# Storing the query projections of later batches ahead of their batches, one of them through the keys' buffer

## The chip, the cores and the metric

The kernel runs on one core of a Trainium2 chip. The metric is the device time of one execution in microseconds (us), the median of several runs. A core has five engines with an instruction queue each, in order: TensorE (PE, matmuls), VectorE (DVE), ScalarE (ACT), GpSimd (POOL) and SyncE (SP), which here issues nearly all DMA transfers. An engine whose next instruction waits holds up everything queued behind it on that engine, and on SyncE that means transfers that could have gone.

## The reference

Two blocks follow each other. The first is a linear attention with sketched features for 4 batches of 4 heads, 1088 positions and 32 dimensions; the second is a mixture of 8 experts over the 4352 rows (4 x 1088) that come out of it, weighted by 8 rounds of a row and column normalisation.

```python
def phi(x):                                   # S1, S2: 8 x 32
    a = einsum('rd,bhsd->bhsr', S1, x)
    b = einsum('rd,bhsd->bhsr', S2, x)
    return einsum('bhsi,bhsj->bhsij', a, b).reshape(..., 64)
q_p, k_p = phi(q), phi(k)
kv = einsum('bhsf,bhsd->bhfd', k_p, v);  z = sum(k_p, axis=2)
x = einsum('bhsf,bhfd->bhsd', q_p, kv) / (einsum('bhsf,bhf->bhs', q_p, z) + 1e-6)
# x as (4352, 128): batch and position x head and dimension
P = exp(x @ w_gate - max)
for _ in range(8):
    P /= P.sum(1) + 1e-9;  P /= P.sum(0) + 1e-9;  P *= N / E
out = sum over e of P[:, e] * (maximum(x @ w1[e], 0) @ w2[e])
```

## The kernel before

**Attention.** Batch 0 takes a short way of its own: its query features are made by two matmuls that repeat both factors in PSUM (`query_products`, `multiply`), and sums and quotients follow in three chunks of positions (`fractions`, `divide`). Batches 1 to 3 go through DRAM. `transpose_q(b)` turns the loaded queries in 32x32 blocks on VectorE into the single buffer `qT`. `queries_ab(b)` multiplies `qT` with both sketches (L418, 12 records on TensorE, into two PSUM banks), ScalarE copies the product to `qab` (one buffer, L421), and SyncE stores it to DRAM twice: as `qa` (L425) and as `qb` (L429). `repeat_a(b)` reads `qa` back, each row repeated, into `ph` (two buffers, batch b uses `phs[b % 2]`, L434), and `repeat_b(b)` reads `qb` back into `rb` (one buffer, L437). `times(b, c)` multiplies the two on VectorE, in thirds (L444), `tops(b, c)` contracts them with the sums of the keys on TensorE (L453, L457), and `over(b, c)` divides on VectorE. `take_over(b, ...)` then stores the result to DRAM (`xd<-xt`, L477) and reads it back in its other layout into `xT` (`xT<-xd`, L479), from where the experts take it.

The keys take a similar way without DRAM: `transpose_k(b)` into `kT` (L292, L294), `keys_ab(b)` (L303, L307, TensorE and a ScalarE copy), `keys_products(b, part)` on VectorE (L319), `keys_sums(b)` on TensorE (L335), `keys_kept(b)` into `kvs`.

**Experts.** The first layer is a step of two matmuls into one bank of PSUM (`first`, L889) and a ReLU on ScalarE (L893) into `hb`; a step's two halves run beside each other on TensorE. VectorE forms differences of hidden blocks (L906), and the second layer follows eight steps later (`into`, L1062); 7 products stand for 8 block products, or 20 for a larger form, in the way of fast matrix multiplication. The unweighted work of experts 0 and 1 runs first, group by group: 16 steps each on columns of batch 0 (256, 288 and 256 wide), then three groups of width 480 that start with the columns of batch 1, and so on; all others wait for the routing weights.

**What sets the order.** `fill(n)` lays down expert steps from a generator until n units are spent (a unit is a step of 480 columns; a step of 256 is 0.533). Attention and routing are written out by hand with `fill` between their parts, under a manual order for VectorE and TensorE, and at the very start for ScalarE too:

```python
def fill(n):
    owed[0] += n
    while owed[0] > 0.25:
        owed[0] -= next(work)
...
        for b in range(1, B):
            for n, _ in zip((1.4,) * (9 if b + 1 < B else 5), attention(b), strict=True):
                fill(n)
```

After the start, ScalarE and SyncE are ordered by a scheduler, so what stands ahead of what on these two follows from when it supposes things to be ready. Four PSUM banks (tag `a`) serve first-layer steps, `tops`, the keys and the query projections alike. A program-wide set of eight DMA semaphores is used in turn, and a transfer waits for the one that used its semaphore before.

Of the kernel before, what the change touches and what calls it, by code (L numbers as in the profile page):

```python
# [10 lines left out]
F32 = mybir.dt.float32  # L11
# [39 lines left out]
def kernel(  # L51
# [12 lines left out]
    nc = tc.nc  # L64
    P = nc.NUM_PARTITIONS
# [59 lines left out]
    xT = big.tile([P, N + 2 * 32], F32, name="xT")  # L125

    W9 = 9 * 32
    qT = wk.tile([P, 4 * W9], F32, name="qT", bufs=1)
    nc.gpsimd.memset(qT[:, S:], 0.0)
    kT = wk.tile([P, S], F32, name="kT", bufs=1)  # L130

    phs = [wk.tile([P, 2, 4 * W9], F32, name=f"ph{i}", bufs=1) for i in range(2)]
    rb = wk.tile([P, 2, 4 * W9], F32, name="rb", bufs=1)

    lgT = qT[:, 0:S].rearrange("p (a s) -> p a s", s=32)
    lgp = kT.rearrange("p (a e) -> p a e", e=32)
    pT = dram.tile([E, N], F32, name="pT")


# [24 lines left out]
    def load_q(b):  # L164
        qx = ld.tile([P, SA, D], F32, tag="q", name="qx")
        nc.sync.dma_start(out=qx, in_=q[b].rearrange("h (s a) d -> (h s) a d", a=SA))
        loaded["q", b] = qx

    def load_v(b):
        vx, o = v_slots[b % 2], v[b].offset  # L170
        for c in range(4):
            nc.sync.dma_start(
                out=vx[32 * c:32 * (c + 1), 0:H, 0:NT, :].rearrange("p h t d -> p h (t d)"),
                in_=AP(tensor=v.tensor, offset=o + NT * D * c, ap=[[SA * D, 32], [S * D, H], [1, NT * D]]))
        for c in range(2):
            nc.sync.dma_start(
                out=vx[32 * c:32 * (c + 1), 0:H, NT, :],
                in_=AP(tensor=v.tensor, offset=o + (4 * NT + c) * D, ap=[[SA * D, 32], [S * D, H], [1, D]]))

    load_k(0)  # L180
    load_q(0)
    load_v(0)

    def load_w(e, sums=True, again=False):
        w1 = wpool.tile([P, F], F32, tag="w1", name="w1")
# [92 lines left out]
    nc.gpsimd.memset(wg, 0.0)  # L278
    nc.sync.dma_start(out=wg[:, 0:E], in_=moe_w_gate)
    first_w = load_w(0)  # L280
    load_q(1)
    load_v(1)


    keys, queries = {}, {}

    def transpose_q(b, lo=0, hi=S):
        nc.vector.transpose(out=qT[:, lo:hi], in_=loaded["q", b].rearrange("p a d -> p (a d)")[:, lo:hi])

    def transpose_k(b):  # L290
        kx = loaded["k", b]
# [50 lines left out]
    def keys_kept(b):  # L342
        pv = sums_of.pop(b)
        for s in range(2):
            sl = slice(64 * s, 64 * (s + 1))
            if b:
                x, y = kvs[b % 2][sl, :, s, :], pv[sl].rearrange("p i c d -> p i (c d)")[:, :, 0:D + 1]
            else:
                x, y = kvz[sl, :, :, s, :], pv[sl].rearrange("p i c d -> p c i d")
            if s:  # L350
                nc.vector.tensor_copy(x, y)
            else:
                nc.scalar.copy(x, y)
# [55 lines left out]
    def queries_ab(b):  # L409
        qa = dram.tile([H * R, 2, 2, 2 * W9], F32, name=f"qa{b}")  # L410
        qb = dram.tile([2, R, 2 * R, 2, 2 * W9], F32, name=f"qb{b}")
        ab = wk.tile([P, 3, 192], F32, tag="qab", name="qab", bufs=1)
        x = qT.rearrange("p (h q c t s) -> p h c t q s", h=2, q=2, c=3, t=3)
        for cs in ((0, 1), (2,)):
            pq = bank()[:, 0:192 * len(cs)].rearrange("p (c n) -> p c n", n=192)
            for i, c in enumerate(cs):
                for s in range(2):
                    nc.tensor.matmul(pq[64 * s:64 * (s + 1), i].rearrange("p (t q s) -> p t q s", t=3, q=2),  # L418
                                     wdq.rearrange("p n f -> p (n f)"), x[:, s, c], start=True, stop=True,
                                     tile_position=(0, 64 * s))  # L420
            nc.scalar.copy(ab[:, cs[0]:cs[-1] + 1], pq)  # L421
        abf = ab.rearrange("p c n -> p (c n)")
        for s in range(2):
            x = abf[64 * s:64 * s + 32].unsqueeze(1).to_broadcast([32, 2, 2 * W9])
            nc.sync.dma_start(out=qa[:, :, s], in_=x)  # L425
        for s in range(2):
            for h in range(2):
                x = abf[64 * s + 32 + h:64 * (s + 1):2].unsqueeze(1).to_broadcast([2 * R, R, 2 * W9])
                nc.sync.dma_start(out=qb[h, :, :, s].rearrange("i f n -> f i n"), in_=x)  # L429
        queries[b] = qa, qb  # L430

    def repeat_a(b):
        for j in range(4):
            nc.sync.dma_start(out=phs[b % 2][j::4], in_=queries[b][0].rearrange("(x r) j s n -> (r j) x (s n)", x=2))  # L434
# [11 lines left out]
    def tops(b, c):  # L446

        pn = bank()[:, 0:3 * H * (D + 1)].rearrange("p (t h d) -> p t h d", t=3, h=H)
        ph = third(phs[b % 2], c)
        for t in range(3):  # L450
            for i in range(2):
                for s in range(2):
                    nc.tensor.matmul(pn[64 * s:64 * (s + 1), t, 2 * i:2 * i + 2].rearrange("p h d -> p (h d)"),  # L453
                                     ph[:, i, s, 64 * t:64 * (t + 1)], kvs[b % 2][:, i].rearrange("p h d -> p (h d)"),
                                     start=(t == 0 and i == 0), stop=False, tile_position=(0, 64 * s))
        for s in range(2):
            nc.tensor.matmul(pn[64 * s:64 * (s + 1), :, :, D], ones[:, 0:64], eps, start=False, stop=True,  # L457
                             tile_position=(0, 64 * s))
        queries[b, c] = pn
# [14 lines left out]
    def take_over(b, lo, hi):  # L474

        xd = dram.tile([P, H, hi - lo], F32, name=f"xd{b}{lo}")
        nc.sync.dma_start(out=xd, in_=turned[b][:, :, lo:hi])  # L477
        for h in range(H):
            nc.sync.dma_start(  # L479
                out=xT[32 * h:32 * (h + 1), b * S:b * S + 4 * W9].rearrange("d (f n) -> d f n", f=4)[:, :, lo:hi],  # L480
                in_=xd.rearrange("(f d) h n -> h d f n", f=4)[h])
# [16 lines left out]
    def attention(b):  # L498


        follows = b + 1 < B
        keys_sums(b)
        times(b, 0)
        if follows:
            transpose_q(b + 1)
        yield
        keys_kept(b)
        if follows:
            queries_ab(b + 1)
            repeat_a(b + 1)  # L510
        times(b, 1)
        tops(b, 0)
        yield
        times(b, 2)
        if follows:
            repeat_b(b + 1)
        over(b, 0)
        tops(b, 1)
        yield
        over(b, 1)  # L520
        if b + 1 == B:
            take_over(b, 0, 192)
        yield
        tops(b, 2)
        if follows:
            transpose_k(b + 1)
        if b + 2 < B:
            load_k(b + 2)
            load_q(b + 2)
            load_v(b + 2)  # L530
        yield
        over(b, 2)
        if b + 1 < B:
            take_over(b, 0, W9)
        else:
            take_over(b, 192, W9)
        if follows:
            keys_ab(b + 1)
            yield
            keys_products(b + 1, 0)  # L540
            yield
            keys_products(b + 1, 1)
            yield
            keys_products(b + 1, 2)
            yield
# [589 lines left out]
    with tc.manual_schedule(engines={engines.DVE, engines.PE, engines.Activation}):  # L1135
        st = projections()
        transpose_k(0)
        keys_ab(0)
        repeated(st)
        load_k(1)  # L1140
        transpose_q(0, 0, chunks[0][1])
        query_products(0)
        for part_ in range(3):
            keys_products(0, part_)
        keys_sums(0)
        multiply(0)
        transpose_q(0, chunks[0][1])
        keys_kept(0)
        query_products(1)
        fractions(0)  # L1150
        multiply(1)
        divide(0)
        fractions(1)
        query_products(2)
        divide(1)
    with tc.manual_schedule(engines={engines.DVE, engines.PE}):
        fill(1)
        multiply(2)
        fractions(2)
        fill(1)  # L1160
        transpose_q(1)
        queries_ab(1)
        repeat_a(1)
        repeat_b(1)
        fill(1)
        divide(2)
        fill(1)
        transpose_k(1)
        load_k(2)
        load_q(2)  # L1170
        load_v(2)
        fill(1)
        keys_ab(1)
        fill(1.5)
        keys_products(1, 0)
        fill(1.5)
        keys_products(1, 1)
        fill(1.5)
        keys_products(1, 2)
        fill(1.5)  # L1180
        for b in range(1, B):
            for n, _ in zip((1.4,) * (9 if b + 1 < B else 5), attention(b), strict=True):
                fill(n)
        for n in routing():
            fill(n)
        early.close()
        pools.append(ctx.enter_context(tc.tile_pool(name="late", bufs=2)))
        prepare_x(PLAIN)
        fill(8)
# [32 lines left out]
```

## Time and profile before

| | |
|---|---|
| time, median of 3 | 937.68 us (936.96 to 938.76) |
| span of the profiled execution | 935.3 us, TensorE clock 0.998 |
| TensorE (PE) busy | 914.8 us |
| VectorE (DVE) busy | 696.3 us |
| ScalarE (ACT) busy | 416.6 us |
| moved by DMA | 128.14 MB, mean 137 GB/s |
| `rb<-qb`, 1152 KB, issue to landing | 8.0 us (median of 3) |
| `qx<-in_q`, 544 KB | 5.3 us |
| `xT<-xd`, 144 KB | 3.3 us |

Busy times are sums over the span, and the ends of matmuls are modelled, so a busy TensorE need not be at its peak. A line of a timeline gives the start, the length, engine and line of the kernel, what is written from what, the count, and in brackets the idle time before it and what ended it. A wait for several things is put down to the one that came last by the profile, which can be the wrong one where a DMA was among them.

### The profile page before, as it was taken

To read this page: it belongs to the slowest core of one execution; us is meant where nothing else is said; L and a number is where in the kernel's file an instruction comes from. 1 tells how busy PE (TensorE), PEld (TensorE's weight loads), DVE (VectorE), ACT (ScalarE), POOL (GpSimd) and SP (SyncE) were. 2 spreads that over 40 slices of the span, in tenths; PEclk is the share of its full clock that TensorE was granted. 3 is DMA by queue.
4 is the path that set the end of the run, shared out by engine and by line. 5 is a ranking of instruction groups with operands and counts; after the bars stand their busy time and mean duration, and the time that the engine had idled before them with its cause. 6 is when DMAs were issued, how large, how long until landed. Compare 5 with 4: busy or idle time off the path is not lost.

```text
span 935.3 us, 18858 instructions
## 1 busy us (share of the span) xinstructions
PE 914.8 (98%) x7434; PEld 556.6 (60%) x7434; DVE 696.3 (74%) x1200; ACT 416.6 (45%) x901; POOL 195.9 (21%) x182
## 2 busy tenths in 40 slices
PE   8888999999999999999999999999999999999997
PEld 6676634666666666665555555555555555556864
DVE  7687769978788788586876656965757977768655
ACT  2544345564444454434544444544445444445443
POOL 2010000073665501130020101201110343321210
PEclk9999999999999999999999999999999999999999
DMA  7896300123335545354354534364434446442640
GB/s 216 226 290 166 113 21 1 26 105 108 107 109 170 172 148 151 121 174 142 117 154 121 179 107 148 111 182 131 140 115 152 151 150 204 160 167 92 183 140 12
DMA packets 93208, 128.14 MB, mean 137 GB/s; under 512 B 25376, under 2 KB 71456, under 8 KB 88384
## 3 DMA queue, kind: packets, MB, share of 16 engines
q1 hardware_dynamic: 91888, 126.78, 43.8%
q8 instruction: 58, 0.95, 0.4%
q10 hardware_dynamic: 1232, 0.16, 0.1%
q14 instruction: 30, 0.25, 0.1%
HBM read 107.88 MB, written 19.05 MB: 136 GB/s over the span
## 4 chain that ended last, share of the span: by engine, by line
PE 90%; DVE 8%; issue 1%; ACT 1%; POOL 0%; DVEq 0%; ACTq 0%; POOLq 0%
PE a L889 47%; PE s L1062 40%; DVE hb L906 2%; PE a L335 1%; PE a L114 1%; PE a L303 0%; PE a L453 0%; DVE rs L582 0%; DVE ph L444 0%; DVE p L585 0%; DVE cs L588 0%; DVE kp L319 0%; DVE kept L715 0%; DVE w L718 0%; DVE kT L292 0%
## 5 line engine op out<-in xcount | busy, mean ns | idle before, releaser
L889 PE MATMUL a<-xe,w 128*64 128x256 f32 (+1 forms) x2560 | 517.5, 470 | 0.0
L893 ACT ACTIVATE hb<-a 128x256 f32<-128x256 f32 (+5 forms) x408 | 194.9, 479 | 253.5 <-PE a L889 225.0
L893 ACT ACTIVATE hx<-a 128x256 f32<-128x256 f32 (+1 forms) x360 | 167.1, 464 | 213.9 <-PE a L889 194.1
L889 PEld LDWEIGHTS a<-xe,w 128*64 128x64 f32 x2560 | 206.8, 137 | 79.8
L1062 PE MATMUL s<-hb,ws 128*64 128x256 f32 (+4 forms) x1344 | 237.8, 395 | 2.4 <-DVE hb L906 1.6
L1062 PE MATMUL s<-hx,ws 128*64 128x256 f32 x1280 | 204.8, 379 | 0.6 <-DVE kept L718 0.6
L951 DVE TENSOR_TENSOR hb<-hb 128x512 f32<-128x512 f32 (+1 forms) x204 | 133.4, 665 | 93.9 <-ACT hb L893 89.8
L951 DVE TENSOR_TENSOR hx<-hx 128x512 f32<-128x512 f32 (+1 forms) x204 | 153.3, 761 | 66.3 <-ACT hx L893 61.1
L658 POOL TENSOR_TENSOR xe<-xT,xe 128x768 f32<-128x768 f32 (+2 forms) x41 | 85.1, 2076 | 554.5 <-DMA xe<-pT 401.6
L1062 PEld LDWEIGHTS s<-hb,ws 128*64 128x64 f32 x1344 | 113.8, 137 | 110.6 <-issue 80.0
L1062 PEld LDWEIGHTS s<-hx,ws 128*64 128x64 f32 x1280 | 105.9, 137 | 99.7 <-issue 74.4
L889 PE MATMUL a<-xT,w 128*64 128x480 f32 (+4 forms) x512 | 119.4, 463 | 3.7 <-DVE hb L906 2.5
L1062 PE MATMUL s<-hb,w 128*64 128x256 f32 (+4 forms) x496 | 101.9, 410 | 0.0
L906 DVE TENSOR_TENSOR hb<-hb 128x480 f32<-128x480 f32 (+8 forms) x96 | 64.2, 670 | 21.1 <-ACT hb L893 13.6
L1062 PE MATMUL s<-hx,w 128*64 128x256 f32 x384 | 68.3, 379 | 0.0
L889 PEld LDWEIGHTS a<-xT,w 128*64 128x64 f32 x512 | 50.5, 137 | 26.6 <-issue 14.2
L238 POOL TENSOR_TENSOR ws<-w 128x256 f32<-128x256 f32 (+1 forms) x70 | 60.1, 892 | 13.6 <-PE a L889 8.7
L1062 PEld LDWEIGHTS s<-hb,w 128*64 128x64 f32 x496 | 45.8, 137 | 22.8 <-issue 8.1
L906 DVE TENSOR_TENSOR hx<-hx 128x256 f32<-128x256 f32 (+1 forms) x65 | 39.1, 607 | 24.5 <-ACT hx L893 23.4
L951 DVE TENSOR_TENSOR pqg<-hb 128x512 f32<-128x512 f32 x68 | 48.8, 759 | 0.0
L1062 PEld LDWEIGHTS s<-hx,w 128*64 128x64 f32 x384 | 34.0, 137 | 10.9 <-DVE hx L906 0.3
L951 DVE TENSOR_TENSOR pqg<-hx 128x512 f32<-128x512 f32 x68 | 35.8, 566 | 0.0
(164 smaller groups left out, 468.8 us busy)
## 6 DMA issues: line engine op xcount, KB each, us to landing
w<-in_moe_w_dram SPq DMA_DIRECT2D x82, 512.0 KB, 5.0
ws<-ws SPq DMA_DIRECT2D x34, 1024.0 KB, 4.9
xe<-pT SPq DMA_DIRECT2D x34, 384.0 KB, 4.0
ws<-ws SPq DMA_DIRECT2D x12, 512.0 KB, 4.9
qb<-qab SPq DMA_DIRECT2D x12, 288.0 KB, 4.2
ph<-qa SPq DMA_DIRECT2D x12, 288.0 KB, 4.4
rb<-qb SPq DMA_DIRECT2D x3, 1152.0 KB, 8.0
pb<-pT SPq DMA_DIRECT2D x6, 384.0 KB, 6.7
```

The source lines that it names most:

```text
L114: nc.tensor.matmul(warm[:, 0:P], ones, ones, start=True, stop=True)
L238: tc.keep_in_program_order(nc.gpsimd.tensor_tensor(ws[:, c:c + len(ns)], blocks(x), blocks(y), op=Alu.subtract if off else Alu.add))
L335: nc.tensor.matmul(pv[64 * s:64 * (s + 1), i], kp[0:n, H * t + h].rearrange("p i j -> p (i j)"), vx[0:n, slots[h], t, :], start=(t == 0 an ...
L658: tc.keep_in_program_order(nc.gpsimd.tensor_tensor(out, x, pb, op=Alu.mult))
L889: nc.tensor.matmul(ph[sl], loaded_w[j][0][:, P * f + H2 * s:P * f + H2 * (s + 1)], sources[j][:, lo:hi], start=True, stop=True, tile_posit ...
L893: nc.scalar.activation(out=out, in_=ph, func=Act.Relu)
L906: nc.vector.tensor_tensor(out, a, b, op=Alu.subtract)
L951: nc.vector.tensor_tensor(out if not isinstance(out, tuple) else places(*out), places(*a), places(*b) if isinstance(b, tuple) else b, op=A ...
L1062: nc.tensor.matmul(sums[g][i][H2 * s:H2 * (s + 1), n * place:n * (place + 1)], w, x, start=c == 1, stop=c == per, tile_position=(0, H2 * s))
```

## The change

Before, the queries of batch b+1 were transposed, projected and stored during attention(b), and those of batch 1 after the last chunk of batch 0 had been multiplied. Now:

- q1 is loaded right after batch 0's data, ahead of the first expert's weights; q2 and q3 are loaded as soon as the two `qx` buffers come free.
- The queries of batch 1 are transposed into `kT`, which is idle between the keys of batch 0 and those of batch 1, and are projected, stored and read back during batch 0.
- The queries of batch 2 are transposed and projected between the key products of batch 1; those of batch 3 in the middle of attention(1), two yields apart.
- With that, the keys of batch 1 come earlier too, and the expert work laid before attention(1) shrinks from 11 units to 5.5.

It is meant to have the data of `ph` and `rb` in place before `times` asks for them.

```diff
-    qT = wk.tile([P, 4 * W9], F32, name="qT", bufs=1)
-    nc.gpsimd.memset(qT[:, S:], 0.0)
-    kT = wk.tile([P, S], F32, name="kT", bufs=1)
+    qT, kT = (wk.tile([P, 4 * W9], F32, name=n, bufs=1) for n in ("qT", "kT"))
+    for t in (qT, kT):
+        nc.gpsimd.memset(t[:, S:], 0.0)
...
     load_k(0)
     load_q(0)
     load_v(0)
+    load_q(1)
...
     first_w = load_w(0)
-    load_q(1)
     load_v(1)
...
     def transpose_q(b, lo=0, hi=S):
-        nc.vector.transpose(out=qT[:, lo:hi], in_=...)
+        to = kT if b == 1 else qT
+        nc.vector.transpose(out=to[:, lo:hi], in_=...)
...
-        x = qT.rearrange("p (h q c t s) -> p h c t q s", h=2, q=2, c=3, t=3)
+        x = (kT if b == 1 else qT).rearrange("p (h q c t s) -> p h c t q s", h=2, q=2, c=3, t=3)
...
         keys_sums(b)
         times(b, 0)
-        if follows:
-            transpose_q(b + 1)
         yield
         keys_kept(b)
-        if follows:
-            queries_ab(b + 1)
-            repeat_a(b + 1)
         times(b, 1)
         tops(b, 0)
         yield
...
         over(b, 0)
         tops(b, 1)
+        if b == 1:
+            transpose_q(3)
         yield
         over(b, 1)
         if b + 1 == B:
             take_over(b, 0, 192)
+        if b == 1:
+            queries_ab(3)
         yield
         tops(b, 2)
+        if b == 1:
+            repeat_a(3)
         if follows:
             transpose_k(b + 1)
         if b + 2 < B:
             load_k(b + 2)
-            load_q(b + 2)
             load_v(b + 2)
...
         transpose_q(0, chunks[0][1])
+        load_q(2)
         keys_kept(0)
+        transpose_q(1)
+        load_q(3)
         query_products(1)
         fractions(0)
         multiply(1)
+        queries_ab(1)
+        repeat_a(1)
+        repeat_b(1)
         divide(0)
         fractions(1)
         query_products(2)
         divide(1)
...
-        fill(1)
+        fill(0.5)
         multiply(2)
         fractions(2)
-        fill(1)
-        transpose_q(1)
-        queries_ab(1)
-        repeat_a(1)
-        repeat_b(1)
+        transpose_k(1)
+        load_k(2)
+        load_v(2)
         fill(1)
         divide(2)
+        keys_ab(1)
         fill(1)
-        transpose_k(1)
-        load_k(2)
-        load_q(2)
-        load_v(2)
+        keys_products(1, 0)
         fill(1)
-        keys_ab(1)
-        fill(1.5)
-        keys_products(1, 0)
-        fill(1.5)
         keys_products(1, 1)
-        fill(1.5)
+        transpose_q(2)
+        fill(1)
         keys_products(1, 2)
-        fill(1.5)
+        queries_ab(2)
+        repeat_a(2)
+        fill(1)
```

More of the change, by code (lines that the diff above doesn't have):

```diff
@@ L135 @@
     lgT = qT[:, 0:S].rearrange("p (a s) -> p a s", s=32)
-    lgp = kT.rearrange("p (a e) -> p a e", e=32)
+    lgp = kT[:, 0:S].rearrange("p (a e) -> p a e", e=32)
     pT = dram.tile([E, N], F32, name="pT")
@@ L287, in transpose_q @@
     def transpose_q(b, lo=0, hi=S):
-        nc.vector.transpose(out=qT[:, lo:hi], in_=loaded["q", b].rearrange("p a d -> p (a d)")[:, lo:hi])
+        to = kT if b == 1 else qT
+        nc.vector.transpose(out=to[:, lo:hi], in_=loaded["q", b].rearrange("p a d -> p (a d)")[:, lo:hi])
     def transpose_k(b):
```

## The prediction, made before the result was known

> **What bounds the kernel now.** I read the page first, then the windows of the first 130 us, then TensorE's waits and its timeline, then the timelines of VectorE and of SyncE's DMA queue, since waits seldom start where they show.
>
> ```profile
> PE 914.8 (98%) x7434; PEld 556.6 (60%) x7434; DVE 696.3 (74%) x1200; ACT 416.6 (45%) x901; POOL 195.9 (21%) x182
> ...
> PE 90%; DVE 8%; issue 1%; ACT 1%; POOL 0%; DVEq 0%; ACTq 0%; POOLq 0%
> ```
>
> TensorE is busy nearly throughout, and the chain that ended last is 90% TensorE. The change leaves the matmuls as they are, so it can only give or take TensorE's idle time. Where is that?
>
> ```profile
> 40.00:50.00 10.00, 7.45 (x134) 5.55 (x130) 5.58 (x9) 4.21 (x12) 0.00 (x0) 1.00 1.00 277
> ...
> 80.00:90.00 10.00, 7.45 (x108) 5.07 (x106) 6.20 (x14) 2.67 (x5) 0.00 (x0) 1.00 0.97 253
> ...
> 290.00:300.00 10.00, 10.00 (x79) 6.57 (x76) 9.76 (x11) 4.30 (x9) 9.76 (x11) 1.00 0.01 2
> ```
>
> (PE, PEld, DVE, ACT, POOL busy in each 10 us, then clock, DMA share, GB/s.) It is in the first 90 us, and in two of these windows all DMA engines are busy. What ends the waits:
>
> ```profile
> PE a L889 <- DVE hb L906: 2.5, 1, 2.5
> PE a L303 <- DVE kT L294: 2.3, 2, 1.4
> ...
> PE a L453 <- ACT qab L421: 1.3, 1, 1.3
> PE a L418 <- ACT f L736: 1.2, 1, 1.2
> ```
>
> The timelines (start, length), of VectorE, of TensorE and of SyncE's queue, tell what lies behind:
>
> ```profile
> 43.84 0.96 DVE L444 TENSOR_TENSOR ph<-ph,rb 128x768 f32<-128x768 f32 x1 [5.28 <-DMA rb<-qb]
> 44.72 1.30 DVE L288 STREAM_TRANSPOSE qT<-qx 128x1088 f32<-128x1088 f32 x1
> ```
>
> ```profile
> 46.17 1.20 PE L418 MATMUL a<-qT,wdq 128*64 128x192 f32 x12 [1.25 <-ACT f L736]
> ...
> 83.73 1.03 PE L889 MATMUL a<-xT,w 128*64 128x480 f32 x4 [2.55 <-DVE hb L906]
> ```
>
> ```profile
> 67.72 0.34 SPq L477 DMA_DIRECT2D xd<-xt  x1
> 77.52 0.60 SPq L425 DMA_DIRECT2D qa<-qab  x1
> 78.23 2.41 SPq L479 DMA_DIRECT2D xT<-xd  x4
> ```
>
> First: VectorE waits 5.28 us for `rb` of batch 1, the transpose of q2 stands behind that, and TensorE behind the transpose. Second: batch 1's result is stored (`xd`) at 67.72, but its reload into `xT` is issued only at 78.23, since a store of `qa` that waits for ScalarE stands before it in SyncE's order. The matmul at 83.73 is the first that needs batch 1's columns; its 2.55 us are in truth this DMA, whose landings the trace has 3.2 us after issue, at 82.9 to 83.5.
>
> By matmul starts (a record of 64 columns by 256 streams in 0.107 us: four in 0.43), the gaps from 19 to 84 us sum to about 10 us: 1.0+0.3+0.4+0.2+1.1, then 1.4+1.5 (the `rb` chain), 1.6 (kT of batch 2), 2.8 (xT). That is the most there is to win here.
>
> [...] `xT` sat behind `qa` for 9.8 us. [...] k2, issued after `rb` at 36.03, lands at 46.2, after `rb` at 43.84. [...]
>
> **The change, part by part.**
>
> *Early part, 13 to 40 us.* q1 loads before w1. Its transpose (1.30) fits VectorE's idle 1.35 us before `multiply(1)`: nothing. `queries_ab(1)` is 12 records, 0.96 us, ahead of `fractions(1)`, so TensorE's first expert step moves from 19.1 to 19.9, but `fractions(2)` waited for `multiply(2)` at 21.4 anyway: nothing.
>
> `qab` is ready at 17.9 instead of 25.46. Yet until 24 us the rings still hold k1 (lands at 20.09 before), q2 and now q3 (557 KB each, 2 us each at 280 GB/s). Behind them go qa 0.3, qb 1.15, ph 1.15, rb 1.15 MB: 3.75 MB at the 277 to 286 GB/s of these windows is 13.4 us, so rb lands at about 38, not 43.84: 6 us earlier.
>
> But the expert work laid before attention(1) falls from 11 to 5.5 units. Counted in the two instruction orders up to `tops(1,0)`, that is 10 first-layer steps of 0.43 and 18 second-layer matmuls of 0.21: 8.3 us less TensorE work. VectorE's chain after 21.4 then is: kT 1.43, divide(2) 2.2 (25.05), expert sums and key products 26.15 to 30.1, transpose of q2 to 31.35. TensorE has only five steps meanwhile (25.1 to 27.6), so `queries_ab(2)` waits 3.9 us. Then keys_sums(1), expert steps to 39.0, times(1,0) at 38 to 39, kvs, `tops(1,0)` at about 40. Before: 48.67-8.3=40.4. Equal.
>
> *attention(1), 40 to 64.* Gone is the kT wait (1.6). New: banks. ScalarE's copy of `qab` for batch 3 stands behind keys_sums(2) in its order, so the two PSUM banks of `queries_ab(3)` stay taken from about 47 us to there: with `tops` holding a third, each expert step waits for its own eviction (0.4+0.2 against 0.43 of other matmuls). TensorE's work is 21.8 us (19 steps, 33 second-layer matmuls, 3 tops, keys_ab, queries_ab), VectorE's 22.0; going through it row by row I get 24, so keys_sums(2) begins at 64. Before: 70.94-8.3+1.0 (the extra queries_ab)=63.6. Equal again.
>
> *attention(2): the reload of batch 1.* In the changed SyncE order the `xd` store of batch 1, ready at 55, stands behind qa3, which waits for that same late ScalarE copy (67), then behind qb3, ph3, k3, v3; its reload stands behind rb3, which waits for times(2,2) at 72. From 67: qa to rb issue took 8.9 us for batch 3 of before, k and v 3.7, so `xd` goes at 79.6. By volume, 4.3 MB at 275 GB/s from 67 is 83, so `xd` lands at 84 to 85; then 4 issues of 0.45 and, with rb3's 1.15 MB still ahead (4 us), landing near 90. That is 24 us after the qab copy, against 17.3 of TensorE work (16 steps 6.9, second layer 6.4, tops 2.9, keys_ab 1.2). So the wait for batch 1 grows from 2.75 to about 6.7 us. k3's landing near 80.5 holds keys_ab(3) within it. Bound: if the rings move 300 GB/s and xT overtakes rb3, 86; if issues are held up as the worst k (10.2 us to landing), 93.
>
> TensorE's first 480-wide step is thus at 90.3. Before, brought to the same work (tops(2,2) and keys_ab(3) done): 83.73+2.2=85.9. Loss 4.4 us.
>
> *After that.* Routing ends 5.5 units earlier in the expert work. The two gaps at 170.66 and 178.19 (0.89+0.93) fall where routing meets the group of 192; now it ends about where this group starts. I take 1.0 us gain, 0 to 2 possible. The rest is the same stream of matmuls.
>
> Sum: 937.7+0+0+4.4-1.0=941.1; I take 941.0.
>
> **The rivals.**
>
> *Faster.* The reload is hidden: its data would have to land within 17.3 us of the qab copy. For it: by these estimates the rings have nothing to do from about 60 (rb2 and expert 1's weights in) to 67, so issues start freely; landings took 3.2 us at 78. Against: 4.3 MB stand before it. Then 64+2.4+17.5=83.9 against 85.9: -2; with 1.0 from routing, 934.7.
>
> *Nothing to measure.* The reload lands at 86 to 87, and the early part gives 1: the old 2.75 us wait is traded for one of similar length, 937.7.
>
> *Worse.* The queue of q1, q2, q3 holds `rb` to 42 or more and k1 past 21.4, where VectorE's in-order queue with divide(2), sums and key products stands behind it: 4 us on top, 945.
>
> **How the numbers follow.** The main case gets 0.46, the worse one 0.12, no measurable change 0.17, faster 0.25: the row-by-row passage adds many small terms, each 0.3 us or so uncertain, and the two DMA times 2 to 3 us. Slower is 0.58. The range takes the main case with its bounds (86 gives 937, 93 gives 944) and most of the rivals: 934.0 to 945.5.
>
> **What would show it** (line numbers of the changed kernel are one higher). Right: a first 480-wide L890 step near 90 us with an idle of 4 to 7 us before it; the `xT<-xd` issue of batch 1 after rb3's, later than 80; an idle of 3 to 4 us before L419 near 31; `rb<-qb` landing at 36 to 40; `tops(1,0)` (first L454) near 40. Wrong: if the reload is issued before 76 or that wait is under 3 us, the forecast falls; if L419 of batch 2 hardly waits, the early part gains and the kernel is faster.

## The result and the profile after

The changed kernel takes 953.61 us (median of 4 runs, 953.11 to 954.13), the kernel before, beside it, 937.32 us (936.26 to 938.76): a ratio of 1.0173 with an interval of 1.0155 to 1.019. It is 16.3 us slower, where 3.3 were forecast. The profiled span grew from 935.3 to 952.3 us, and the mean clock of TensorE fell from 0.998 to 0.990.

The page first, where the line of engines and the line of the chain answer to those shown of before:

```profile
PE 918.7 (96%) x7434; PEld 568.4 (60%) x7434; DVE 701.6 (74%) x1200; ACT 416.8 (44%) x901; POOL 195.1 (20%) x183
...
PEclk9997999999999999999999999999999999999999
...
PE 88%; DVE 7%; issue 2%; DMA 1%; ACT 1%; SPq 0%; DVEq 0%; ACTq 0%
```

The same number of matmuls, a little more busy time, and 2% less share. The fourth of the 40 slices (71 to 95 us) has a lower clock, so the search begins there. TensorE's waits (total, times, longest):

```profile
PE s L1063 <- DVE kept L719: 14.5, 2, 13.4
PE a L419 <- DVE qT L289: 3.5, 1, 3.5
```

One wait of 13.4 us holds most of the loss. It is put down to `kept` of L719, a VectorE operation of 0.44 us. That only names what came last, so the next view is VectorE's timeline (start, length, and in brackets the idle time before and its releaser):

```profile
75.55 0.56 DVE L469 TENSOR_TENSOR rd<-a,rc 128x384 f32<-128x384 f32 x1
89.67 0.58 DVE L473 STREAM_TRANSPOSE xt<-rd 128x384 f32<-128x384 f32 x1 [13.56 <-DMA xd<-xt]
90.18 0.84 DVE L907 TENSOR_TENSOR hb<-hb 128x256 f32<-128x256 f32 x2
90.94 0.45 DVE L719 TENSOR_TENSOR z<-s,z 128x288 f32<-128x288 f32 x1
91.30 0.44 DVE L719 TENSOR_TENSOR kept<-s,m 64x288 f32<-64x288 f32 x1
```

VectorE has batch 2's first result in `rd` at 76.11, and wants to transpose it into `xt` (L473). `xt` is one buffer, and what lies in it is batch 1's result, not yet stored. So VectorE waits 13.56 us for a DMA to *read* its own output, and the hidden differences and kept sums of the experts, which have nothing to do with it, wait behind. Why the store is so late is in SyncE's queue (start and length of the issue; x2 means two of them):

```profile
69.95 1.23 SPq L426 DMA_DIRECT2D qa<-qab  x2
71.22 3.61 SPq L430 DMA_DIRECT2D qb<-qab  x4
75.02 4.14 SPq L435 DMA_DIRECT2D ph<-qa  x4
79.27 1.30 SPq L161 DMA_DIRECT2D kx<-in_k_dram  x1
80.62 1.85 SPq L172 DMA_DIRECT2D v<-in_v_dram  x4
82.52 0.90 SPq L176 DMA_DIRECT2D v<-in_v_dram  x2
83.53 0.37 SPq L478 DMA_DIRECT2D xd<-xt  x1
86.61 0.34 SPq L438 DMA_DIRECT2D rb<-qb  x1
89.64 1.74 SPq L480 DMA_DIRECT2D xT<-xd  x4
```

The store `xd<-xt` of batch 1 goes out at 83.53 and lands about 89.6, when VectorE resumes. Its data had been ready since 56.2 (L473 of batch 1 ran from 55.58 for 0.58). It stood behind `qa` of batch 3, and that waited for a copy on ScalarE:

```profile
69.00 0.21 ACT L354 COPY kvs<-a 64x66 f32<-64x66 f32 x1 [3.01 <-PE a L336]
69.22 0.70 ACT L422 COPY qab<-a 128x384 f32<-128x384 f32 x2
```

The copy stands behind the `kvs` copy of batch 2 in ScalarE's order, so it waits for `keys_sums(2)`. SyncE issued nothing from 52.5 to 69.95, and the windows show the DMA engines little used from 60 us on (busy PE, PEld, DVE, ACT, POOL, then clock, DMA share, GB/s):

```profile
60.00:65.00 5.00, 5.00 (x44) 4.06 (x42) 4.95 (x7) 2.46 (x6) 2.79 (x3) 1.00 0.19 52
65.00:70.00 5.00, 4.26 (x88) 3.50 (x86) 4.88 (x7) 1.41 (x6) 1.69 (x2) 1.00 0.01 3
```

From 60 us on, a store that was ready had free DMA engines ahead of it, and could not be issued, because a transfer before it in the queue waited. (The store also takes over the semaphore of the fourth `ph` transfer of batch 3, which landed at about 83.44, so this transfer would have held it just as long.) TensorE's timeline shows the end of it:

```profile
77.64 0.80 PE L890 MATMUL a<-xT,w 128*64 128x256 f32 x3
91.80 0.69 PE L1063 MATMUL s<-hb,w 128*64 128x256 f32 x1 [13.35 <-DVE kept L719]
...
102.22 0.57 PE L890 MATMUL a<-xT,w 128*64 128x480 f32 x1
```

From 78.4 to 91.80 TensorE stands. Then it is slow at first, as windows set at these times show:

```profile
80.00:85.00 5.00, 0.00 (x0) 0.00 (x0) 0.00 (x0) 0.00 (x0) 0.00 (x0) 0.82 0.91 274
85.00:90.00 5.00, 0.00 (x0) 0.00 (x0) 0.33 (x1) 0.00 (x0) 0.00 (x0) 0.50 1.08 303
91.80:94.40 2.60, 2.60 (x12) 1.47 (x14) 2.47 (x6) 0.38 (x1) 0.00 (x0) 0.50 0.82 170
94.40:97.20 2.80, 2.80 (x38) 2.33 (x36) 2.62 (x6) 0.09 (x1) 0.00 (x0) 0.55 0.04 10
97.20:102.20 5.00, 5.00 (x73) 3.99 (x71) 3.59 (x8) 2.43 (x7) 0.00 (x0) 1.00 0.16 65
```

In the 5.4 us after the restart the clock is 0.50, then 0.55. Groups of four matmuls on 256 columns start 0.85 us apart there (92.71, 93.56, 94.41), and 0.43 apart at full clock (100.31, 100.75, 101.18). At those clocks 2.6x0.50 + 2.8x0.55 = 2.8 us worth of matmuls were streamed, so 2.6 us more were lost, with TensorE shown as busy all the time.

The first 480-wide step, which needs batch 1's columns, starts at 102.22. Before it was at 83.73, and brought to the same work, as the prediction did, at 85.9: 16.3 us later, as much as the measured difference. With the stream times of all records summed (an estimate: 0.107 us for one of 64 columns by 256, as four of them start 0.43 us after the four before in the trace of before, at 30.71, 31.14, 31.57 and 32.00; others in proportion), TensorE has lost 16.9 us more than before by 120 us, and some 0.6 us less from 120 to 220 us.

### The profile page after: what moved, and what is told of

It reads as the page before. It is cut to its first block, busy times and chain, and to the rows that moved or that the text cites. A ratio compares the mean times of both kernels' runs of the same rounds, so it can differ in the third digit from the quotient of the medians.

```text
span 952.3 us, 18865 instructions
## 1 busy us (share of the span) xinstructions
PE 918.7 (96%) x7434; PEld 568.4 (60%) x7434; DVE 701.6 (74%) x1200; ACT 416.8 (44%) x901; POOL 195.1 (20%) x183
## 4 chain that ended last, share of the span: by engine, by line
PE 88%; DVE 7%; issue 2%; DMA 1%; ACT 1%; SPq 0%; DVEq 0%; ACTq 0%
PE a L890 46%; PE s L1063 39%; DVE hb L907 2%; DVE kp L320 1%; DMA xd<-xt 1%; PE a L454 1%; PE a L336 1%; DMA ph<-qa 1%; DVE hb L952 1%; PE a L304 0%; PE a L384 0%; ACT hb L894 0%; DVE qT L289 0%; PE s L366 0%; DVE kept L716 0%
## 5 line engine op out<-in xcount | busy, mean ns | idle before, releaser
L890 PEld LDWEIGHTS a<-xe,w 128*64 128x64 f32 x2560 | 213.3, 137 | 73.4 <-issue 1.4
L952 DVE TENSOR_TENSOR hx<-hx 128x512 f32<-128x512 f32 (+1 forms) x204 | 158.1, 785 | 65.9 <-ACT hx L894 60.9
L1063 PEld LDWEIGHTS s<-hb,ws 128*64 128x64 f32 x1344 | 117.0, 137 | 105.0 <-issue 76.4
L1063 PEld LDWEIGHTS s<-hx,ws 128*64 128x64 f32 x1280 | 109.6, 137 | 95.3 <-issue 71.4
L890 PE MATMUL a<-xT,w 128*64 128x480 f32 (+4 forms) x512 | 123.0, 472 | 1.2 <-ACT ab L306 0.6
L907 DVE TENSOR_TENSOR hb<-hb 128x480 f32<-128x480 f32 (+8 forms) x96 | 67.9, 708 | 22.9 <-ACT hb L894 17.1
```

Source lines behind the costliest of these rows:

```text
L890: nc.tensor.matmul(ph[sl], loaded_w[j][0][:, P * f + H2 * s:P * f + H2 * (s + 1)], sources[j][:, lo:hi], start=True, stop=True, tile_posit ...
L907: nc.vector.tensor_tensor(out, a, b, op=Alu.subtract)
L952: nc.vector.tensor_tensor(out if not isinstance(out, tuple) else places(*out), places(*a), places(*b) if isinstance(b, tuple) else b, op=A ...
L1063: nc.tensor.matmul(sums[g][i][H2 * s:H2 * (s + 1), n * place:n * (place + 1)], w, x, start=c == 1, stop=c == per, tile_position=(0, H2 * s))
```

## The experiments

Theory A: `qa` of batch 3 waits in SyncE's queue for ScalarE's late copy, and whatever stands behind it comes late. First the store of batch 1, which holds `xt`, and so VectorE and TensorE. Rivals: B, only the late reload `xT<-xd` counts, as forecast; C, there is too little expert work ahead of attention(1); D, there is too much DMA volume in this stretch, whatever its order. Every run was timed beside the kernel before, and none leaves out any of the computation. The diffs are against the changed kernel where nothing else is said.

**1. Another buffer for batch 2's result.** By the author's reckoning, which no run shows, a second `xt` would not fit beside the rest in SBUF, so batch 2's result goes to `qT`, idle by then. SyncE's order stays.

```diff
-            turned[b] = wk.tile([P, H, W9], F32, tag="xt", name="xt", bufs=1)
+            turned[b] = (qT.rearrange("p (h n) -> p h n", h=H) if b == 2 else
+                         wk.tile([P, H, W9], F32, tag="xt", name="xt", bufs=1))
```

> The transposed result of batch 2 goes into qT, which is idle then, so it no longer shares a buffer with that of batch 1; the order of SyncE's queue stays. Theory A (batch 1's store, late in SyncE's queue, holds the one xt buffer, and VectorE waits for it): the 13.6 us wait of VectorE's transpose goes. As the store and the reload are still issued at 83 to 91 us, the first 480-wide expert step, which could then begin near 86, waits for the reload until about 95: 8 to 9 us of the wait come back there, and the time is 946 to 949. Rival B (the reload alone mattered all along): 953, the same. Rival C (too little expert work before attention of batch 1): 953, the same.

Measured: 948.14 us, ratio 1.0088 (1.0071 to 1.0105). The wait for `xt` is gone. TensorE's waits from 75 to 100 us:

```profile
PE a L304 <- DVE kT L295: 4.2, 1, 4.2
PE a L891 <- DMA xT<-xd: 1.4, 1, 1.4
```

The time is as expected, but not the wait: 8 to 9 us had been expected at the reload. Instead the next transfers of the same queue take its place: the keys of batch 3 (issued at 79.00) hold 4.2 us, the reload 1.4, and the first 480-wide step starts at 95.01. So the hold on `xt`, with the clock it cost, was worth 102.22 - 95.01 = 7.2 us of position in the two traces (5.5 us by the medians of the times). B, by which this change would do nothing, falls as the main cause.

**2. Batch 1's store and reload issued by GpSimd.**

```diff
-        nc.sync.dma_start(out=xd, in_=turned[b][:, :, lo:hi])
+        queue = nc.gpsimd if b == 1 else nc.sync
+        queue.dma_start(out=xd, in_=turned[b][:, :, lo:hi])
...
-            nc.sync.dma_start(
+            queue.dma_start(
```

> Store and reload of batch 1's result are issued by GpSimd, which has nothing to do then, so they stand behind no other transfer; nothing else is changed. Theory A: the store goes at about 58 us and both the wait for xt and the wait for the reload vanish: 936 to 939. Rival B: the same 936 to 939. Rival C: 950 or more, since the expert work is as short as before. Rival D (the many transfers near 70 to 90 us are the limit by their volume, whatever their order): 945 or more, with VectorE waiting for rb or k of batch 3 instead.

Measured: 943.33 us, ratio 1.0037 (1.0024 to 1.005), a miss by 4 us. The store went out at 57.33 and the reload at 65.15, as meant. But TensorE's waits from 75 to 100 us, and the issue in SyncE's queue behind them, are

```profile
PE a L304 <- DVE kT L295: 5.7, 1, 5.7
```

```profile
79.38 0.98 SPq L161 DMA_DIRECT2D kx<-in_k_dram  x1
```

The keys of batch 3 stand behind `qa`, `qb` and `ph` too, and with the store out of the way they are the next to be missed. The expectation had counted only what the store holds.

**3. A second buffer for `qab`** (paid for with one buffer less of `rd`), so that ScalarE's copy for batch 3 need not wait for the stores of batch 2.

```diff
-        ab = wk.tile([P, 3, 192], F32, tag="qab", name="qab", bufs=1)
+        ab = wk.tile([P, 3, 192], F32, tag="qab", name="qab", bufs=2)
```

> A second qab buffer (paid for by one rd buffer less), so that ScalarE's copy for batch 3 need not wait for the stores of batch 2. Theory A with its root in that late copy: the qa store of batch 3 is issued near 50 instead of 70 us, the store of batch 1's result near 62 instead of 83.5, both waits go, and the early release of two PSUM banks gives up to 1 us more: 934 to 938. Rivals C and D: 948 or more.

Measured: 937.49 us, ratio 0.9979 (0.9965 to 0.9994). SyncE's queue:

```profile
50.97 3.75 SPq L426 DMA_DIRECT2D qa<-qab  x2
...
69.08 0.34 SPq L478 DMA_DIRECT2D xd<-xt  x1
```

`qa` goes 19 us earlier, and the store 14 us earlier (62 had been expected for it), and the loss is gone, which C did not expect. On D this run says little: its transfers have moved out of the stretch too (160 GB/s from 70 to 90 us, where the changed kernel has 251).

**4. Batch 3's part alone undone**: its transpose, projection and `repeat_a` go back to attention(2). All else of the change stays.

```diff
+        if b == 2:
+            transpose_q(3)
         yield
         keys_kept(b)
+        if b == 2:
+            queries_ab(3)
+            repeat_a(3)
...
-        if b == 1:
-            transpose_q(3)
...
-        if b == 1:
-            queries_ab(3)
...
-        if b == 1:
-            repeat_a(3)
```

> Only the part of batch 3 is undone: its queries are transposed and projected in attention of batch 2 as before; batches 1 and 2 stay early and the expert work stays short. Theory A: SyncE has no qa3 in front of the store of batch 1, VectorE's wait for xt goes; the reload may again stand behind qa3 for some us as in the kernel before: 937 to 941. Rival C: 950 or more.

Measured: 935.16 us, ratio 0.9942 (0.9926 to 0.9957), faster than the kernel before and than I expected. SyncE's queue:

```profile
63.72 0.34 SPq L478 DMA_DIRECT2D xd<-xt  x1
69.73 0.59 SPq L426 DMA_DIRECT2D qa<-qab  x1
70.43 1.96 SPq L480 DMA_DIRECT2D xT<-xd  x4
```

The store is ahead of `qa`, the first 480-wide step at 83.93. Batch 3's part costs about 18 us by the traces (102.22 - 83.93) and by the times (953.61 - 935.16; 21 if each is taken beside its own runs of before), and the rest of the change gains about 5 (940.03 - 935.16, beside its own runs of before). Here too the other transfers have moved, so D is left to run 9.

**5. The changed kernel with the old 11 units of expert work** ahead of attention(1) (seven `fill` amounts, for instance):

```diff
-        fill(0.5)
+        fill(1)
+        fill(1)
```

> The changed kernel with the old amount of expert work before attention of batch 1 (11 units, not 5.5); all else stays, and SyncE's order still has the store of batch 1 behind qa, qb and ph of batch 3 and k and v of batch 3. Theory A (that order is the loss): VectorE still waits 8 us or more at the transpose of batch 2's result or TensorE for the reload behind it, 947 to 956. Rival C (too little expert work): 934 to 940.

Measured: 943.97 us, ratio 1.004 (1.0024 to 1.0057), 3 us below what A expected, and well above what C did. The order in SyncE's queue stays (`qa` at 62.26, the store at 77.37), and so do the waits, in other sizes. VectorE's, and TensorE's from 70 to 100 us:

```profile
DVE xt L473 <- DMA xd<-xt: 3.6, 1, 3.6
```

```profile
PE a L890 <- DMA xT<-xd: 9.7, 1, 9.7
```

Here it is the reload that ends the longest wait, as the prediction had it. One queue order holds three things (`xt`, the keys, the reload), and how the other work lies beside it decides which shows. C falls as the cause, since about 5 us remain here, and runs 4 and 9 have the short work without the loss; but the amount of work moves the size by 9 to 11 us.

**6. The kernel before with batch 1's part alone** (q1 loaded early, transposed into `kT`, projected and stored during batch 0):

```diff
+        transpose_q(1)
...
+        queries_ab(1)
+        repeat_a(1)
+        repeat_b(1)
         divide(0)
...
-        transpose_q(1)
-        queries_ab(1)
-        repeat_a(1)
-        repeat_b(1)
```

> The kernel before with the part of batch 1 alone: q1 loaded first, turned through kT, projected and stored in batch 0; the expert work, the keys and batches 2 and 3 stay as before. If the gain of the version without batch 3's part is batch 1's: VectorE's wait of 5.3 us for rb goes, and with it the two TensorE waits of 1.4 and 1.5 us near 45 to 49; 935 to 938 where the kernel before gives 938 to 940. If it lies in the earlier projection of batch 2 or in the shorter expert work: within 1 us of the kernel before.

Measured: 935.96 us, ratio 0.9963 (0.9948 to 0.9978). The wait of VectorE for `rb`, and the 1.4 and 1.5 us of TensorE behind it, are gone; waits of 3.1 us for `kT` and 2.4 for `xT` stay.

**7. Run 4, with the queries of batch 2 a step earlier**: transposed right after `divide(2)`, projected after the first key products of batch 1, and two units of expert work at the end in place of one. The difference from run 4:

```diff
+        transpose_q(2)
...
-        keys_products(1, 1)
-        transpose_q(2)
-        fill(1)
-        keys_products(1, 2)
...
+        keys_products(1, 1)
...
+        keys_products(1, 2)
+        fill(2)
```

> Batch 3's part undone as in e4, and batch 2's queries transposed right after the last quotient of batch 0, projected two key products earlier, with one unit more of expert work before attention of batch 1. If TensorE's 3.7 us wait for the transpose of q2 near 27 to 31 us is a real loss: 1.5 to 3 us faster than e4, so 932 to 934. If VectorE's key products take its place as the bound there: the same as e4.

Measured: 929.18 us, ratio 0.9896 (0.9866 to 0.9925), better than both kernels, and twice the gain that was expected over run 4. The 3.5 us before L419 are gone; TensorE's longest waits up to 130 us are now

```profile
PE a L454 <- ACT qab L422: 1.0, 1, 1.0
PE a L114 <- POOL own L116: 1.0, 1, 1.0
PE a L304 <- DVE kT L293: 0.7, 1, 0.7
```

The first 480-wide step is at 78.83, 5.1 us ahead of run 4, against 6.0 us in the times. The expectation had counted the wait alone, and not the clock behind it. The same stretch in run 4 and in this run:

```profile
29.60:36.40 6.80, 5.44 (x30) 3.83 (x32) 3.38 (x6) 0.77 (x2) 0.00 (x0) 0.50 0.90 317
```

```profile
29.60:36.40 6.80, 6.75 (x112) 4.96 (x110) 2.58 (x6) 2.09 (x6) 0.00 (x0) 1.00 0.97 322
```

Run 4 has 5.44 us of matmuls at half clock, so 2.7 us lost beside the wait of 3.5 us.

**8. Run 4 with the old 11 units** of expert work, by the same amounts as in run 5:

```diff
-        fill(0.5)
+        fill(1)
+        fill(1)
```

> Batch 3's part undone as in e4, and the old 11 units of expert work before attention of batch 1. Theory: with the long expert work TensorE does not wait for the transpose of q2, and rb comes in time, so only the reload's wait may be left: 932 to 936, 0 to 3 us faster than e4. Rival C gives the same number here but not in e5, where the order of SyncE's queue is kept.

Measured: 935.8 us, ratio 0.9959 (0.9948 to 0.9971), within 0.6 us of run 4. With the order mended, the amount of expert work hardly matters.

**9. Run 2, and the keys of batch 3 issued by GpSimd as well**, all the rest of the changed order kept:

```diff
-        nc.sync.dma_start(out=kx, in_=k[b].rearrange("h (s a) d -> (h s) a d", a=SA))
+        (nc.gpsimd if b == 3 else nc.sync).dma_start(out=kx, in_=k[b].rearrange("h (s a) d -> (h s) a d", a=SA))
```

> As e2, and k of batch 3 too is issued by GpSimd, early, so that neither the result of batch 1 nor the keys of batch 3 stand behind qa, qb and ph of batch 3 in SyncE's queue. Theory A, extended by what e2 showed (whatever stands behind qa of batch 3 comes late, and there it was k of batch 3, for which TensorE waited 5.9 us): that wait goes too, 935 to 939, some 5 us faster than e2. Rival D (volume of the transfers): 942 to 945 as in e2, with VectorE waiting for k or rb all the same.

Measured: 936.26 us, ratio 0.997 (0.9959 to 0.998). This is all that is left of TensorE's waits from 60 to 100 us:

```profile
PE a L454 <- ACT hb L895: 0.5, 1, 0.5
```

The queues of SyncE and of GpSimd:

```profile
69.06 1.23 SPq L426 DMA_DIRECT2D qa<-qab  x2
```

```profile
56.38 0.56 POOL L479 DMA_DIRECT2D xd<-xt  x1 [4.66 <-DVE xt L473]
```

And the stretch from 70 to 90 us, in the changed kernel and in this run:

```profile
70.00:90.00 20.00, 8.45 (x114) 6.26 (x109) 4.78 (x9) 6.05 (x16) 0.00 (x0) 0.83 0.92 251
```

```profile
70.00:90.00 20.00, 19.98 (x251) 14.65 (x249) 17.77 (x34) 10.36 (x27) 1.63 (x2) 1.00 0.87 249
```

`qa` of batch 3 is as late as ever, and the DMA engines move as much in this stretch (249 and 251 GB/s). Only the store with its reload, and the keys, no longer stand behind it, and about 17 us (953.0 - 936.3) come back. D falls with this, and A is shown: the blocked order, and neither volume nor the early part, is the loss. For the store, the issue from GpSimd took away the time for which it was blocked in SyncE's queue: 83.53 - 56.38 = 27 us.

**10. The changed kernel again**, beside run 9:

> The changed kernel once more, beside e9 and the kernel before on the same chip, as the measure for both: 952 to 955, a ratio of 1.015 to 1.019.

Measured: 952.99 us, ratio 1.0149 (1.0115 to 1.0184), a hair under the expected ratio, since the kernel before came out at 938.86 us here (23 executions): the loss is 14.1 us in this comparison, 16.3 in the first.

## Why the prediction was wrong

The direction and the place were right: the store and the reload of batch 1 behind `qa` of batch 3, and that behind a late ScalarE copy. The size was not, and the time fell outside the range.

- *Early part*: held, but for the clock. The wait before L419 of batch 2 was 3.54 us, ending at 31.31 (forecast 3.9, 31.35). `rb` landed at 35.9 (38). `tops(1,0)` began at 41.49 (40), so "equal" was 1.5 us off. Behind the wait TensorE ran at half clock for 3.4 us, busy throughout (the lines are in the last section). That costs 1.7 us, about what the forecast of this part lacked.
- *attention(1)*: `keys_sums(2)` began at 65.32 (64), some 1.3 us late, which the step before brought along.
- *attention(2), the step that failed.* The queue was forecast in its order, and late by a few us only: `qab` copied from 69.22 (67), `xd` issued at 83.53 (79.6), the reload landed near 95 (90). (The forecast was not quite of one piece: its works sum to 17.4 us, given as 17.3 and 17.5, and from 67 to 90 are 23 us, not 24.) What failed is "so the wait for batch 1 grows from 2.75 to about 6.7 us": it hung the cost on the reload, the last thing in the chain. The store before it held `xt`, which L473 of batch 2 needs at 76.11, long before the reload is wanted. The working asked who waits for what the store *writes*, not who waits for the buffer that it *reads*. So 13.35 us of TensorE's time went where none was counted. With all its work 16.3 us later, TensorE came to the 480-wide steps at 102.22, after the reload had landed, and the reload cost nothing.
- *The keys*: "k3's landing near 80.5 holds keys_ab(3) within it" failed too: they landed near 86.6, and with `xt` freed (run 1) they alone hold 4.2 us. Of the 11.9 us between the forecast of the first 480-wide step (90.3) and its start (102.22), run 1 gives 7.2 to `xt` and the clock. The other 4.7 stay in run 1. Its waits for the keys and the reload (4.2 and 1.4) with 2.9 us of half clock behind the keys (5.85 us of matmuls at 0.50, from 86.1 to 92.9) are 1.8 more than the 6.7 forecast, and the later start of attention(2) is 1.3; the remaining 1.6 are not attributed.
- *The clock*: not forecast at all. 1.7 us in the early part, and 2.6 after the long wait, included in the 7.2.
- *After that*: some 0.6 us gained from 120 to 220 us, where 1.0 was taken (0 to 2 possible).

The sum, now from measured terms: 65.32 for `keys_sums(2)`, 19.9 of work from there on (the prediction's 2.4 + 17.5), 13.35 of waiting and 2.6 of clock give 101.2, where the trace has 102.22. About 1 us is spread over smaller waits and not attributed.

Of the rivals, *worse* looked at the early queue, which ran as in the main case. The range took the bounds of the landing times, 86 to 93, as its ends, but no bound for a wait that had not been seen.

One reading of the lines of before was too large: the 9.8 us for which `xT` sat behind `qa` run from the issue of the store, which itself took about 5.2 us to land (67.72 to 72.95), so the reload was held for some 4.6.

Two things stay open. Why the scheduler put the copy of batch 3 behind `kvs` of batch 2 was not traced further than that a second `qab` buffer, with `rd` cut to one, changes it. And a real second `xt` buffer was not tried.

## What to carry to other kernels

When a DMA issue moves back in its queue, list both sides of each transfer behind it: who waits for what it writes, and who waits to overwrite what it reads; with a single buffer the second can come first. Taking away one wait in such a queue shows the next (`xt`, then the keys, then the reload, 13.4, 4.2 and 1.4 us), so count all that stands behind the blocked issue before forecasting what a repair brings. And a transfer that is ready should not share an in-order queue with one that waits for a late producer: move the late one behind it (run 4, the store at 63.72 in place of 83.53), make its producer early (run 3, at 69.08), or issue what is ready from another engine (run 9, at 56.38).

## What was not expected of the hardware

An idle TensorE cost more here than its idle time. It stopped at 78.4; a mean clock of 0.82 in 80 to 85 and 0.50 after, if it fell once from 1.0 to 0.5, puts the fall at 83.2, 4.8 us after the stop. It restarted at 91.80, and 0.55 in 94.4 to 97.2 puts the rise at 96.9, 5.1 us after. In run 1 (mean clock 0.81 in 80 to 90, 0.85 in 90 to 100), with the stop at 82.9, the fall at 86.1, the restart at 87.05 and the rise at 92.9, the delays are 3.2 and 5.9 us; what sets them is not shown. In the changed kernel this cost 2.6 us on top of 13.35.

Far shorter waits were followed by half clock too. Around the wait of 3.54 us before L419, the changed kernel has

```profile
28.63:32.04 3.41, 0.73 (x10) 0.77 (x12) 3.41 (x5) 0.00 (x0) 0.00 (x0) 1.00 0.98 350
32.04:35.45 3.41, 3.41 (x20) 2.54 (x18) 0.87 (x3) 0.42 (x2) 0.00 (x0) 0.50 0.97 330
```

and lost 1.7 us in the second stretch. TensorE was not idle throughout before the clock fell: it was busy for 0.73 of the 3.41 us. In run 8 a wait of 1.9 us ended at 60.83, and TensorE ran at half clock behind it until 63.5: a group of four matmuls on 256 columns started 0.85 us before the next one there (62.67 to 63.52), and 0.43 us just after (64.01 to 64.44). That is some 1.3 us lost, half of 2.7. The kernel before had a wait of 2.55 us, up to 83.73, with a clock of 1.00 from 80 to 90 us. So waits of 1.9 to 3.5 us cost from nothing (before) to 2.7 us more (run 4, in run 7's section), and a forecast should have a range for it. The spread between executions of one kernel goes with the clock as well: beside run 10 the kernel before took from 935.34 us at a mean clock of 0.999 to 942.44 us at 0.993.
